# Gated linear attention and a feed-forward layer on one core: queries laid with d at partitions from the third chunk, V fetched in halves, due times of their own for chunks and weights

## The chip, the cores and the metric

One core of a Trainium2 chip runs the whole program. The metric is device microseconds of one launch. The kernel before took 511.89 us (median of 3 runs, 510.52 to 512.65). Five engines work side by side: TensorE (PE), VectorE (DVE), ScalarE (ACT), GpSimd (POOL) and SyncE (SP, which here only issues transfers). Each runs its own instructions in the order in which the program was written.

## The reference

```python
# q, k, v, alpha: (4 batches, 8 heads, 768 tokens, 48); w_in (384, 2048), w_out (2048, 384); float64 weights
for t in range(S):
    state = alpha[:, :, t, :, None] * state + einsum('bhd,bhe->bhde', k[:, :, t], v[:, :, t])
    y[:, :, t] = einsum('bhd,bhde->bhe', q[:, :, t], state)
x = y.transpose(0, 2, 1, 3).reshape(B * S, H * D)        # 3072 tokens x 384
h = x @ w_in
g = where(h >= 1, h, where(h <= -1, 0, (h + 1) ** 2 / 4))
out = g @ w_out
```

## The kernel before

The 3072 tokens are cut into 24 chunks of 128 (six to a batch). A chunk is prepared (`prepare`), attended (`attend`: `begin_chunk`, `scores`, `update`, `follow`, `outputs`, `end_chunk`) and then goes, three chunks at a time (a group, 384 columns), through the feed-forward layer: `hidden` makes the first product of a block f of 128 hidden units (nine matmuls, L912) and the activation, `second` the second product (nine matmuls, L983). There are 8 groups and 16 blocks. Both products are made of three float32r products (high x high, high x low, low x high), so operands are split into a high part (a cast on ACT) and a low part (a subtraction on DVE or POOL). The weights arrive as 64-bit words and are decoded by ACT (L368, L376, L421), DVE (L384, L395) and POOL or DVE (L408, L423); the set u serves blocks 2u and 2u+1. The first two groups share the weights: blocks 0 to 7 of group 0, the same of group 1, then blocks 8 to 15 of both.

Preparing chunk j: a, k and q are loaded (`load`, L470). The scan along time needs d at partitions. For j < EARLY = 7 the arrays are read with tokens at partitions (`tok_a`, `tok_k`, `tok_q`) and PE turns them into PSUM (`turned`, L485: four matmuls for each of a, k, q); from chunk 7 on they are read with d at partitions (`dim_...`) into SBUF. DVE scans a forward into Q (L546) and backward into inv (L572), multiplies inv by k (L588); the product Q times q (L598) is made by DVE where q lies in PSUM (chunks 1 to 6) and by POOL elsewhere, since POOL doesn't read PSUM. The keys are turned for the state's update: by PE (L662) before TURN = 10, by DVE and a round trip through DRAM (L617, L628, L638) from there. `scores` (L675) and `update` (L688, keys times V) are 32 and 32 small matmuls, `outputs` (L815) 32 to 48. V comes twice: `vt` with all heads (L507) for the update, and `both` (L518), which holds V of the other half of the chunk in 64 partitions and the state in the other 64, for the outputs. `both` has two buffers, and POOL clears it at the start (L266). `place` copies the state into `both` (ACT L707 or POOL L710). From MERGE = 6 the update and scores of chunk j and the outputs of chunk j-1 are one burst on PE.

The order on each engine is written by a planner (`Plan`): every step has an engine, an estimated duration, and a key (due time, in units of one block of a group); at each point the step that can start first goes, and of those the one with the lowest key. Some steps name a second engine (`other`). Where the planner sees PE idle for over 0.45 it puts matmuls on zeros (L1054).

Of the kernel before, what the change touches and what calls it, by code (L numbers as in the profile page):

```python
# [8 lines left out]
F32 = mybir.dt.float32  # L9
# [20 lines left out]
TURN = 10  # L30
PLACING = 4.0
MORE = 2
WARM = 15
LAG = 3.0
FETCH = 12.0
LOAD = 4.0
DECODE = 3.0
PREPARE = 2.5
MARGIN = 9.0
MARGIN0 = 9.0  # L40
MARGIN1 = 5.0
FETCH0 = 18.0
DECODE0 = 10.0
AHEAD = 15.0
FIRST = 5
ROOM = 2
LATER = 8.0
MERGE = 6
WARMTH = 165.0
HALVES = 5  # L50
QHELP = 1
HELP = 4
# [3 lines left out]
ALONE = 2  # L56

# [177 lines left out]
def gated_attention_ffn(ctx: ExitStack, tc: tile.TileContext, q, k, v, alpha, laid, out):  # L235
# [29 lines left out]
    both = const.tile([P, 2, 2, 2, G, 64], F32, name="both")  # L265
# [47 lines left out]
    with ExitStack() as main:  # L313
# [121 lines left out]
        def weights(u):  # L435
# [4 lines left out]
            fetch = key - (FETCH if u else FETCH0)  # L440
            ready = key - (DECODE if u else DECODE0)
# [13 lines left out]
            decode(u, "o", to, wo[u], ready + LAG)  # L455
# [4 lines left out]

        raws = {}

        def load(x, j, key):

            raw = raws[x, j] = buf("stage", "raw", [P, G * CH], 8)
            plan.op(
                "SP",
                Plan.ISSUE,
                key,
                lambda: nc.sync.dma_start(out=raw(), in_=laid[("tok_" if j < EARLY else "dim_") + x][j]),  # L470
                [],
                [raw],
                moved=P * G * CH * 4,
            )

        def turned(x, j, key, to=()):

            raw = raws[x, j]
            if j < EARLY:
# [17 lines left out]
        def prepare(j, key):  # L497

            early = j < EARLY
            for x in "akq":  # L500
                load(x, j, key - LOAD)
            vt = V[j] = buf("vp", "vt", [P, H, D], 2)
# [4 lines left out]
                lambda: nc.sync.dma_start(out=vt().rearrange("p h d -> p (h d)"), in_=laid["v"][j]),  # L507
                [],
                [vt],
                moved=P * DM * 4,  # L510
            )
            for r in range(2):
# [49 lines left out]
            vec(  # L562
                0.13,
                lambda: nc.vector.tensor_copy(out=inv()[:, G - 1, CH - 1 : CH], in_=bwd[:, G - 1, CH - 1 : CH]),  # L564
                ["bwd"],
                [inv],
                False,
            )
# [22 lines left out]
                j >= EARLY,  # L591
# [91 lines left out]
        def update(j):  # L683
            for g in range(G):
                for u in range(1 + ((j + 1) % PER != 0)):
                    for r in range(2):
# [4 lines left out]
                            rhs=V[j]()[halves[u], 2 * g + r],  # L691
# [4 lines left out]
        def place(i, u, key, zero=False):  # L696

            for r in range(2):
                to = both[low[r], i, r, u, :, 0:D]
                if zero:  # L700
                    plan.op("POOL", 0.15, key, lambda to=to: nc.gpsimd.memset(to, 0.0), [], [("s", i, u, r)])
                    continue
                plan.op(
                    "ACT",
                    0.36,
                    key,
                    lambda r=r, to=to: nc.scalar.copy(out=to, in_=state[low[r]]),  # L707
                    ["state"],
                    [("s", i, u, r)],
                    other=("POOL", 0.38, lambda r=r, to=to: nc.gpsimd.tensor_copy(out=to, in_=state[low[r]]), True),  # L710
                )
# [8 lines left out]
        def follow(j, key):  # L720
# [3 lines left out]
            i = j % 2  # L724
# [81 lines left out]
        def outputs(j, ps):  # L806
            n, i = group_of[j], j % 2
# [16 lines left out]
        def used(j):  # L824
            i = j % 2
# [43 lines left out]
        def attend(j, key):  # L869
# [5 lines left out]
            if j > MERGE:  # L875
                ps = ps_a(j)

                def burst(ps=ps):
# [5 lines left out]
                    "PE", 2.2, key, burst, [Q, K, ks, vt, *used(j - 1)], [*meets[j], others[j], ps], mode="quad", ends="col"  # L884
                )
                end_chunk(j - 1, ps, key)
            else:
                o = plan.op("PE", 0.55, key, lambda: scores(j), [Q, K], [*meets[j], others[j]], mode="quad")
                plan.op("PE", 0.55, key + 0.02, lambda: update(j), [ks, vt], meets[j], mode="quad", beside=True, after=[o])
# [5 lines left out]
            if (j + 1) % PER:  # L895
                place((j + 1) % 2, 0, key + 0.2)
# [164 lines left out]
        for j in range(NCH):  # L1061
# [3 lines left out]
            prepare(j, due - PREPARE - PLACING * (j >= TURN))  # L1065
# [159 lines left out]
def lay(q, k, v, alpha, w_in, w_out):  # L1225
# [57 lines left out]
```

## Time and profile before

| | |
|---|---|
| median of 3 runs | 511.89 us |
| profiled execution | 511.24 us, its span 509.5 us |
| PE busy | 494.9 us (97%) |
| DVE, ACT, POOL busy | 308.7, 312.8, 214.2 us |
| chain that ended last | PE 86%, DVE 10%, ACT 1%, issue 1% |
| granted TensorE clock | 0.998 over the span |

The shares are means over very different stretches. PE is fed by itself over most of the span; in the first 80 us DVE is at 0.9 or more of nearly every slice, and the transfers too.

### The profile page before, as it was taken

What the parts mean: (1) busy time and instruction counts of PE and PEld (TensorE: products, weight loads), DVE (VectorE), ACT (ScalarE), POOL (GpSimd) and SP (SyncE); (2) the same over time, 40 slices, a digit from 0 to 9 for tenths busy, and PEclk for the clock granted to TensorE, in tenths of its full rate; (3) what the DMA queues carried; (4) which work ended last, traced back from release to release, by engine and by line L of the source; (5) the groups of instructions that cost most, each with busy time, mean ns of one, the idle gap of its engine ahead of it and who ended that gap; (6) DMA issues with size and microseconds to landing.
All of it is one profiled execution on the core that took longest, in us unless ns stands there. A gap on an engine that the chain in (4) does not pass through costs nothing.

```text
span 509.5 us, 12191 instructions
## 1 busy us (share of the span) xinstructions
PE 494.9 (97%) x4839; PEld 477.8 (94%) x4839; DVE 308.7 (61%) x599; ACT 312.8 (61%) x611; POOL 214.2 (42%) x250
## 2 busy tenths in 40 slices
PE   8898989999999999999999999999999999999995
PEld 6787879999999999999999999999999999999994
DVE  6989998898996737457457457457457413121112
ACT  3898797786655545656555655556555655555551
POOL 3664633432255345444445434445345332333330
PEclk9999999999999999999999999999999999999999
DMA  8997957021355744344234433343213301010001
GB/s 250 376 360 234 371 166 269 9 73 53 106 170 118 218 104 120 80 116 158 58 101 129 122 105 119 77 111 122 59 37 66 110 2 21 4 48 1 0 2 51
DMA packets 59486, 59.80 MB, mean 117 GB/s; under 512 B 33600, under 2 KB 43296, under 8 KB 59424
## 3 DMA queue, kind: packets, MB, share of 16 engines
q1 hardware_dynamic: 59424, 58.97, 39.1%
q8 instruction: 40, 0.66, 0.5%
q14 instruction: 22, 0.18, 0.1%
HBM read 47.32 MB, written 9.57 MB: 112 GB/s over the span
## 4 chain that ended last, share of the span: by engine, by line
PE 86%; DVE 10%; ACT 1%; issue 1%; DVEq 0%
PE ps L983 38%; PE ps L912 38%; PE ps L815 4%; PE ps L688 2%; PE ps L675 2%; DVE inv L572 2%; DVE Q L546 2%; DVE wt L423 1%; DVE Q L761 1%; PE ps L662 1%; DVE w L395 1%; DVE inv L588 1%; PE ps L1054 1%; DVE ps L955 1%; DVE gh L962 0%
## 5 line engine op out<-in xcount | busy, mean ns | idle before, releaser
L912 PE MATMUL ps<-ring,wt 128*128 128x384 f32 (+1 forms) x1170 | 224.5, 336 | 1.1 <-DVE gh L962 1.1
L983 PE MATMUL ps<-wt,gh 128*128 128x384 f32 x1152 | 224.3, 339 | 0.0
L912 PEld LDWEIGHTS ps<-ring,wt 128*128 128x128 f32 x1170 | 204.8, 188 | 1.5 <-DVE gh L962 1.2
L983 PEld LDWEIGHTS ps<-wt,gh 128*128 128x128 f32 x1152 | 201.1, 188 | 1.4 <-POOL gh L962 0.2
L962 POOL TENSOR_TENSOR gh<-gf,gh 128x384 fp32r<-128x384 f32 x101 | 109.3, 1082 | 169.6 <-ACT gh L961 169.6
L955 DVE SCALAR_TENSOR_TENSOR gf<-gf,ps 128x384 f32<-128x384 f32 x102 | 56.2, 551 | 153.1 <-ACT gf L941 150.2
L941 ACT ACTIVATE gf<-ps,half_b 128x384 f32<-128x384 f32 (+1 forms) x130 | 75.0, 577 | 89.9 <-PE ps L912 88.6
L961 ACT CAST gh<-gf 128x384 fp32r<-128x384 f32 x102 | 52.3, 513 | 66.5 <-DVE gf L955 66.5
L941 ACT ACTIVATE gf<-gf 128x384 f32<-128x384 f32 (+1 forms) x130 | 67.7, 520 | 3.9
L408 POOL TENSOR_TENSOR w<-w,wt 128x384 int32<-128x384 int32 (+1 forms) x26 | 32.0, 1246 | 41.1 <-DVE w L395 12.9
L792 POOL TENSOR_TENSOR state<-state,last 128x192 f32<-128x192 f32 x20 | 18.6, 930 | 33.8 <-DVE state L717 33.6
L761 DVE TENSOR_TENSOR Q<-ps,mask 64x256 f32<-64x256 f32 x48 | 20.3, 423 | 14.2 <-ACT other L725 13.2
L815 PE MATMUL ps<-Q,both 128*64 128x64 f32 x372 | 26.8, 225 | 0.8 <-DVE inv L572 0.8
L815 PE MATMUL ps<-other,both 128*64 128x64 f32 x372 | 26.8, 225 | 0.0
L815 PEld LDWEIGHTS ps<-Q,both 128*64 128x64 f32 x372 | 23.5, 138 | 3.3 <-DVE inv L572 1.0
L598 POOL TENSOR_TENSOR Q<-Q,raw 128x512 f32<-128x512 f32 x18 | 23.3, 1294 | 5.0 <-DVE inv L564 2.4
L707 ACT COPY both<-state 48x192 f32<-48x192 f32 x62 | 21.6, 349 | 3.1 <-DVE state L715 0.8
L815 PEld LDWEIGHTS ps<-other,both 128*64 128x64 f32 x372 | 23.5, 138 | 0.0
L572 DVE TENSOR_TENSOR_SCAN inv<-raw,bwd 128x511 f32<-128x511 f32 x17 | 23.0, 1355 | 0.0
L546 DVE TENSOR_TENSOR_SCAN Q<-raw,fwd 128x512 f32<-128x512 f32 x17 | 20.8, 1224 | 0.2
L962 DVE TENSOR_TENSOR gh<-ps,gh 128x384 fp32r<-128x384 f32 (+1 forms) x28 | 14.6, 524 | 6.7 <-ACT gh L961 6.7
L688 PEld LDWEIGHTS ps<-vt,ks 64*64 64x64 f32 x704 | 13.3, 134 | 5.1 <-issue 4.6
(79 smaller groups left out, 447.8 us busy)
## 6 DMA issues: line engine op xcount, KB each, us to landing
both<-in_laid_v_both SPq DMA_DIRECT2D x48, 128.0 KB, 3.0
wt<-in_laid_w_in SPq DMA_DIRECT2D x8, 768.0 KB, 7.4
wt<-in_laid_w_out SPq DMA_DIRECT2D x8, 768.0 KB, 7.5
vt<-in_laid_v SPq DMA_DIRECT2D x24, 192.0 KB, 2.8
out<-ot SPq DMA_DIRECT2D x24, 192.0 KB, 2.6
raw<-in_laid_dim_a SPq DMA_DIRECT2D x17, 256.0 KB, 2.7
raw<-in_laid_dim_k SPq DMA_DIRECT2D x17, 256.0 KB, 2.7
raw<-in_laid_dim_q SPq DMA_DIRECT2D x17, 256.0 KB, 2.6
```

The lines of the kernel that those rows point to most:

```text
L408: add = lambda e, c=c: e.tensor_tensor(out=bits()[:, c], in0=bits()[:, c], in1=word(I32, 0)[:, c], op=ALU.add)
L546: lambda: nc.vector.tensor_tensor_scan(flat(Q()), aT(), flat(fwd), 0.0, ALU.mult, ALU.max),
L572: lambda: nc.vector.tensor_tensor_scan(flat(inv())[:, 0:n][:, ::-1], aT()[:, 1 : n + 1][:, ::-1], flat(bwd)[:, 0:n][:, ::-1], bwd[:, G - 1 ...
L688: nc.tensor.matmul(out=up(j, u)[64 * r : 64 * r + 64, g], lhsT=turnt[j]()[halves[u], g, 64 * r : 64 * r + 64], rhs=V[j]()[halves[u], 2 * g ...
L761: lambda r=r, u=u, to=to: nc.vector.tensor_tensor(out=to()[halves[1 - r], :, halves[u]], in0=ss(j, r)[halves[u]], in1=mask[halves[u], None ...
L815: nc.tensor.matmul(out=ps()[halves[r], to, halves[u]], lhsT=lhsT[:, r, u], rhs=x()[:, g, halves[u]], start=m + u == 0, stop=True, skip_gro ...
L912: nc.tensor.matmul(out=h(), lhsT=win(f, w)[:, kt], rhs=ring[:, at, kt, a, :], start=(m == 0), stop=(m == 3 * KT - 1),)
L941: lambda: nc.scalar.activation(out=gf(), in_=in_(), func=func, scale=scale, bias=bias),
L955: lambda: nc.vector.scalar_tensor_tensor(out=x(), in0=gf(), scalar=1.0, in1=h(), op0=ALU.min, op1=ALU.max),
L961: plan.op("ACT", 0.08 + (0.45 if x is h else 0.41) * w, key + 0.4, lambda: nc.scalar.copy(out=gh()[:, 0], in_=x()), [x], [gh])
L962: sub = lambda e: e.tensor_tensor(out=gh()[:, 1], in0=x(), in1=gh()[:, 0].bitcast(F32), op=ALU.subtract)
L983: nc.tensor.matmul(out=o_ps[seg][t](), lhsT=gh()[:, a, (t - c0) * CH : (t - c0 + 1) * CH], rhs=wout(f, w), start=(f == f0 and i == 0), sto ...
```

## The change

The loads of q switch to d at partitions from chunk 2 on (EARLYQ = 2) instead of chunk 7; a and k stay as they were (EARLYK = EARLY = 7). So the four PE transposes of q fall away for chunks 2 to 6, and Q times q of these chunks goes from DVE to POOL. The token rows that are still loaded hold 464 numbers instead of 512 (neighbouring heads overlap). `vt` holds, for each half of the tokens, only the heads that `both` doesn't hold there (96 KB instead of 192 KB), and the update reads the other half of V from `both`, which therefore gets three buffers (NB) and a longer clearing. TURN falls from 10 to 9, MERGE and HELP rise by one (HELP: chunks whose second mask is made by ACT and POOL), weight decoding on POOL is no longer split in halves (HALVES = 0). The remaining numbers move keys: SHIFT and PREP for single chunks, WFETCH, WREADY and WOUT for single weight sets. In the diff, L numbers of the changed kernel are 10 to 13 higher than those above.

```diff
+EARLYK = 7
+NB = 3
+EARLYQ = 2
-TURN = 10
-PLACING = 4.0
+TURN = 9
+PLACING = 3.0
...
-LATER = 8.0
-MERGE = 6
+LATER = 4.0
+MERGE = 7
 WARMTH = 165.0
-HALVES = 5
+HALVES = 0
 QHELP = 1
-HELP = 4
+HELP = 5
...
+SHIFT = {0: -3.0, 1: -0.5, 6: -1.0, 7: -1.5, 8: 4.5, 9: 1.0, 10: 5.5, 11: 1.5}
+WREADY = {0: -4.5, 1: 0.5, 2: -0.5, 3: -1.0, 4: 0.5, 5: -0.5, 6: -1.5}
...
-    both = const.tile([P, 2, 2, 2, G, 64], F32, name="both")
+    both = const.tile([P, NB, 2, 2, G, 64], F32, name="both")
...
+        WIDE = (G - 1) * (64 + D) + P
+        TOK = {"a": EARLY, "k": EARLYK, "q": EARLYQ}
...
-                lambda: nc.sync.dma_start(out=raw(), in_=laid[("tok_" if j < EARLY else "dim_") + x][j]),
+                lambda: nc.sync.dma_start(
+                    out=raw()[:, 0:WIDE] if j < TOK[x] else raw(), in_=laid[("tok_" if j < TOK[x] else "dim_") + x][j]
+                ),
...
-            if j < EARLY:
+            if j < TOK[x]:
...
-                            in_=raw()[:, g * P : (g + 1) * P],
+                            in_=raw()[:, g * (64 + D) : g * (64 + D) + P],
...
-            vt = V[j] = buf("vp", "vt", [P, H, D], 2)
+            vt = V[j] = buf("vp", "vt", [P, G, D], 2)
...
-            in_ps = QHELP <= j < EARLY
+            in_ps = QHELP <= j < EARLYQ
             ways = [("DVE", 0.66, lambda: mul(nc.vector), not in_ps), ("POOL", 1.3, lambda: mul(nc.gpsimd), True)]
-            (e, us, emit, port), other = ways if QHELP <= j < EARLY else reversed(ways)
+            (e, us, emit, port), other = ways if QHELP <= j < EARLYQ else reversed(ways)
...
-                            rhs=V[j]()[halves[u], 2 * g + r],
+                            rhs=V[j]()[halves[u], g] if r == u else both[halves[u], j % NB, r, u, g, 0:D],
...
-            prepare(j, due - PREPARE - PLACING * (j >= TURN))
+            due += SHIFT.get(j, 0.0)
+            prepare(j, due - PREPARE - PLACING * (j >= TURN) - PREP.get(j, 0.0))
```

On DVE, this is chunk 3 in preparation in the kernel before, from its first gate (fwd) to the products by k (inv) and q (Q), and what follows (w is a weight set being decoded, ring the split outputs of a chunk):

```order
L536 TENSOR_SCALAR fwd<-ps 128x4
L543 MEMSET ps 128x4
L546 SCALAR_TENSOR_TENSOR Q<-ps,fwd 128x512
L717 TENSOR_TENSOR state<-state,ps 128x192
L550 RECIPROCAL bwd<-Q 128x4
L564 COPY inv<-bwd 128x1
L572 SCALAR_TENSOR_TENSOR inv<-ps,bwd 128x511
L584 RECIPROCAL meet<-inv 128x4
L588 TENSOR_TENSOR inv<-inv,ps 128x512
L598 TENSOR_TENSOR Q<-Q,ps 128x512
L844 TENSOR_TENSOR ring<-ps,ring 128x3x128
L395 SCALAR_TENSOR_TENSOR w<-wt,w 128x768
```

And the same chunk on DVE in the changed kernel (L561 and L585 are the scans, L601 the product by k):

```order
L551 TENSOR_SCALAR fwd<-ps 128x4
L558 MEMSET ps 128x4
L561 SCALAR_TENSOR_TENSOR Q<-ps,fwd 128x512
L727 TENSOR_TENSOR state<-state,ps 128x192
L394 TENSOR_SCALAR w<-w 128x768
L565 RECIPROCAL bwd<-Q 128x4
L577 COPY inv<-bwd 128x1
L585 SCALAR_TENSOR_TENSOR inv<-ps,bwd 128x511
L854 TENSOR_TENSOR ring<-ps,ring 128x3x128
L597 RECIPROCAL meet<-inv 128x4
L405 SCALAR_TENSOR_TENSOR w<-wt,w 128x768
L394 TENSOR_SCALAR w<-w 128x768
```

The product by q is gone from DVE, the product by k follows only behind this piece, and the first weight set is decoded here; in the kernel before its first step stood 21 rows ahead of the piece.

On POOL the products by q of chunks 4 and 5 now stand among the decoding of the first two weight sets, each behind a low part or an addition of full width (768 columns). Before, POOL had only `last` of these chunks there, and the first sets went in halves of 384 columns.

On ACT, this follows the ninth high part of a block (L961) in the kernel before, up to the tenth:

```order
L961 CAST gh<-ps 128x384
L421 CAST wt<-w 128x768
L941 ACTIVATE gf<-ps,half_b 128x384
L941 ACTIVATE gf<-gf 128x384
L368 ACTIVATE w<-wt 128x768
L542 COPY meet<-fwd 128x4
L368 ACTIVATE w<-wt 128x768
L376 ACTIVATE wt<-wt 128x768
L961 CAST gh<-ps 128x384
```

And in the changed kernel, from the ninth to behind the eleventh (L971 is the cast; L378, L386 and L431 decode):

```order
L971 CAST gh<-ps 128x384
L431 CAST wt<-w 128x768
L951 ACTIVATE gf<-ps,half_b 128x384
L951 ACTIVATE gf<-gf 128x384
L386 ACTIVATE wt<-wt 128x768
L971 CAST gh<-ps 128x384
L951 ACTIVATE gf<-ps,half_b 128x384
L951 ACTIVATE gf<-gf 128x384
L378 ACTIVATE w<-wt 128x768
L971 CAST gh<-ps 128x384
L386 ACTIVATE wt<-wt 128x768
```

Of the sixteen L376 steps 14 stand before the ninth cast and 2 between it and the eighteenth in the kernel before; 9 and 7 in the changed one. Of the L421 steps it is 7 and 4 before, 6 and 5 now.

## Rows read from the trace of the kernel before

**Rows 1.** Stretches: length, busy us of PE, PEld, DVE, ACT, POOL; clock, DMA share, GB/s
```profile
5.00:73.00 68.00, 60.63 (x955) 52.80 (x953) 62.92 (x133) 55.74 (x109) 35.02 (x51) 1.00 0.90 299
73.00:100.00 27.00, 26.93 (x183) 26.60 (x184) 23.29 (x48) 21.35 (x41) 9.72 (x14) 1.00 0.51 171
...
130.00:504.00 374.00, 373.43 (x3432) 366.14 (x3430) 194.88 (x375) 211.00 (x418) 156.07 (x169) 1.00 0.31 83
```
**Rows 2.** Chain of waits, 0 to 84 us: start, us, what
```profile
52.20 1.15 PE ps L815 x32
...
69.14 0.66 PE ps L662 x4
...
72.54 0.48 DVE gh L962
...
73.06 1.85 PE ps L912 x9
74.92 0.61 PE ps L688 x32
```
**Rows 3.** Groups of DVE, 10 to 80 us: count, busy, mean ns
```profile
L598 DVE TENSOR_TENSOR Q<-Q,ps 128x512 f32<-128x512 f32 x6 | 4.1, 680 | 0.0
```
**Rows 4.** Timeline of DVE, 30 to 82 us: start, us
```profile
32.55 0.68 DVE L598 TENSOR_TENSOR Q<-Q,ps 128x512 f32<-128x512 f32 x1
33.15 0.55 DVE L844 TENSOR_TENSOR ring<-ps,ring 128x384 fp32r<-128x384 f32 x1
...
49.45 0.86 DVE L761 TENSOR_TENSOR other<-ps,mask 64x256 f32<-64x256 f32 x2
```
**Rows 5.** Timeline of PE, 97 to 105 us
```profile
99.14 0.60 PE L662 MATMUL ps<-ident,inv 128*128 128x128 f32 x4
99.50 1.81 PE L983 MATMUL ps<-wt,gh 128*128 128x384 f32 x9
...
102.82 0.68 PE L688 MATMUL ps<-vt,ks 64*64 64x48 f32 x32
...
104.99 0.44 PE L983 MATMUL ps<-wt,gh 128*128 128x384 f32 x1
```
**Rows 6.** Timeline of ACT, 10 to 75 us
```profile
44.57 0.83 ACT L421 CAST wt<-w 128x768 fp32r<-128x768 f32 x1
...
59.33 1.74 ACT L376 ACTIVATE wt<-wt 128x768 int32<-128x768 uint32 x2
```
**Rows 7.** Groups of POOL over the span
```profile
L598 POOL TENSOR_TENSOR Q<-Q,raw 128x512 f32<-128x512 f32 x18 | 23.3, 1294 | 5.0 <-DVE inv L564 2.4 <-PE ps L675 1.9 <-ACT raw L596 0.5
...
L408 POOL TENSOR_TENSOR w<-w,wt 128x768 int32<-128x768 int32 x6 | 11.5, 1909 | 20.1 <-ACT ks L665 8.6 <-ACT gf L941 7.6 <-DVE w L395 4.0
```
**Rows 8.** The line L588: duration ns min/median/max
```profile
L588 DVE TENSOR_TENSOR inv<-inv,raw x17: 691/1112/1683, 85.0 to 391.5; 128x512 f32<-128x512 f32 x17
L588 DVE TENSOR_TENSOR inv<-inv,ps x7: 686/689/689, 8.8 to 68.4; 128x512 f32<-128x512 f32 x7
```
**Rows 9.** Timeline of POOL, 0 to 90 us
```profile
1.02 1.80 POOL L266 MEMSET both<- 128x2048 f32 x1
2.86 0.29 POOL masks.py:199 TENSOR_SCALAR_AFFINE_SELECT ident<-ident 128x128 f32<-128x128 f32 x1
```
**Rows 10.** Timeline of SP, 0 to 6 us (issues)
```profile
2.85 1.21 SPq L518 DMA_DIRECT2D both<-in_laid_v_both  x2
4.11 0.59 SPq L470 DMA_DIRECT2D raw<-in_laid_tok_a  x1
```
**Rows 11.** Timeline of PE, 0 to 12 us
```profile
1.06 3.38 PE L1054 MATMUL ps<-zeros 128*128 128x256 bf16 x15 [1.06 <-DVE zeros L249]
4.24 2.67 PE L485 MATMUL ps<-ident,raw 128*128 128x128 f32 x12
...
8.81 1.28 PE L485 MATMUL ps<-ident,raw 128*128 128x128 f32 x8 [0.37 <-DMA raw<-in_laid_tok_a]
```

More of the change, by code (lines that the diff above doesn't have):

```diff
@@ L506, in prepare @@
                 key - LOAD + 1,
[L507 removed]
+                lambda: nc.sync.dma_start(out=vt().rearrange("p g d -> p (g d)"), in_=laid["v"][j]),
                 [],
                 [vt],
[L510 removed]
+                moved=P * DM * 2,
             )
@@ L518, in prepare @@
                     lambda r=r, rows=rows: nc.sync.dma_start(
-                        out=both[rows, j % 2, r].rearrange("p u g e -> p (u g e)"), in_=laid["v_both"][j, rows]
+                        out=both[rows, j % NB, r].rearrange("p u g e -> p (u g e)"), in_=laid["v_both"][j, rows]
                     ),
                     [],
-                    [("v", j % 2, u) for u in range(2)],
+                    [("v", j % NB, u) for u in range(2)],
                     moved=P * DM * 4 * 2 // 3,
@@ L561, in prepare @@
             )
[L562 to L568, printed above, removed]
+            last_col = lambda e: e.tensor_copy(out=inv()[:, G - 1, CH - 1 : CH], in_=bwd[:, G - 1, CH - 1 : CH])
+            if TAIL and early:
+                plan.op("POOL", 0.22, key, lambda: last_col(nc.gpsimd), ["bwd"], [inv], port=True)
+            else:
+                vec(0.13, lambda: last_col(nc.vector), ["bwd"], [inv], False)
             n = G * CH - 1
@@ L702, in place @@
                     continue
[L703 to L711, printed above, removed]
+                ways = [
+                    ("ACT", 0.36, lambda r=r, to=to: nc.scalar.copy(out=to, in_=state[low[r]]), False),
+                    ("POOL", 0.38, lambda r=r, to=to: nc.gpsimd.tensor_copy(out=to, in_=state[low[r]]), True),
+                ]
+                (e, us, emit, port), other = reversed(ways) if key < PLACE else ways
+                plan.op(e, us, key, emit, ["state"], [("s", i, u, r)], port=port, other=None if key < PLACE else other)
         def grow(j, u, key):
@@ L883, in attend @@
                 plan.op(
-                    "PE", 2.2, key, burst, [Q, K, ks, vt, *used(j - 1)], [*meets[j], others[j], ps], mode="quad", ends="col"
+                    "PE", 2.2, key, burst, [Q, K, ks, vt, ("v", j % NB, 0), ("v", j % NB, 1), *used(j - 1)], [*meets[j], others[j], ps], mode="quad", ends="col"
                 )
@@ L895, in attend @@
             if (j + 1) % PER:
-                place((j + 1) % 2, 0, key + 0.2)
+                place((j + 1) % NB, 0, key + 0.2)
         def hidden(n, f, key, c0=0, c1=GROUP):
@@ L1237, in lay @@
         x = x.reshape(B, H, S // CH, CH, D)[..., e]
-        laid["tok_" + name] = x.transpose(0, 2, 3, 1, 4).reshape(NCH, CH, H * 64)
+        t = x.transpose(0, 2, 3, 1, 4).reshape(NCH, CH, G, 2 * 64)
+        laid["tok_" + name] = np.concatenate([t[:, :, :-1, : 64 + D].reshape(NCH, CH, -1), t[:, :, -1]], axis=2)
         x = x.reshape(B, G, 2, S // CH, CH, 64)
         laid["dim_" + name] = x.transpose(0, 3, 2, 5, 1, 4).reshape(NCH, P, G * CH)
-    x = v.reshape(B, H, S // CH, CH, D)
-    laid["v"] = x.transpose(0, 2, 3, 1, 4).reshape(NCH, CH, DM)
+    x = v.reshape(B, G, 2, S // CH, 2, HC, D)
+    x = np.stack([x[:, :, u, :, u] for u in range(2)], axis=3)
+    laid["v"] = x.transpose(0, 2, 3, 4, 1, 5).reshape(NCH, CH, G * D)
     x = v.reshape(B, G, 2, S // CH, 2, HC, D)[:, :, ::-1].transpose(0, 3, 2, 5, 4, 1, 6).reshape(NCH, P, 2, G, D)
```

41 lines of the change are left out of this document (23 added, 18 removed).

## The prediction, blind

> **What bounds the kernel now.** I read the slices first, then the busy time by stretches, then the chain of waits, then the timelines where the chain leaves PE. The reader is to see two regimes. From about 73 us on PE is busy for 26.93 of 27.0 us and then for 373.43 of 374.0 [rows 1]: no wait is left there, and only PE's own work or a new wait can change the time. Before, from 5 to 73 us, PE is busy for 60.63 of 68 us, part of it on zeros, while DVE is busy for 62.92 [rows 1]. That is 93%, and the chain shows that it is DVE that PE waits for: the eighth block's first product stands at 73.06 because its PSUM bank is freed by the low part that DVE makes at 72.54 (L962), and the keys at 69.14 wait for DVE's product by k in the same way [rows 2]. The first product at 73.06 is the last one with a wait ahead of it in the chain; call it the gate. What moves the gate moves the end, unless the dense stretch behind it loses it again. ACT has 55.74 us of the 68 and POOL 35.02: POOL has room, ACT a little. The clock is 1.00 in all three stretches [rows 1], the upper of TensorE's two levels, so no gain or loss is looked for there.
>
> **Part by part.** All sums are made against the profiled execution, 511.24 us, which is 0.65 below the median of 511.89 and within the runs shown.
>
> *Products by q.* Six of them stand on DVE before [rows 3], one in the changed order (chunk 1). One runs 680 ns, but the next DVE instruction starts 0.60 us behind it (32.55 to 33.15 [rows 4]); so 5 x 0.60 = 3.0 us leave DVE ahead of the gate. *Second masks* of chunk 4 (HELP): two instructions of 0.43 [rows 4], 0.87 us. Counted through the order, these seven are what DVE has less up to the tenth block's low part for good; one scan and one subtraction of a weight set are only put off behind it, and I count no gain for them. DVE is busy 93% of the time, so nearly all of the 3.9 us should reach the gate: **-3.9 us**. From both sides: 0 if other waits take the place, and up to -9.0 if the 5.1 us in which DVE stands idle (68 less 62.92) went too.
>
> *PE's transposes of q.* Twenty matmuls fewer, all ahead of the gate, where PE waits for DVE or runs on zeros. DVE's relief already holds the gain, so they count nothing more.
>
> *PE behind the gate.* In the changed order the update of chunk 6 stands ahead of the gate; in the old one it comes right behind it (0.61 us at 74.92 [rows 2]). The outputs of chunk 6 come out of the burst with chunk 7: before, the burst of update, scores and outputs takes 2.17 us (102.82 to 104.99 [rows 5]); now the outputs alone take 1.15 (52.20 [rows 2]) and update and scores the other 1.02. So that part stays at 2.17, and the 0.61 us go. The keys of chunk 9 leave PE (TURN): 0.36 us (99.14 to 99.50 [rows 5]). Together **-1.0 us**, since PE has no idle time there.
>
> *What comes in for the keys of chunk 9* is one more DVE transpose and five more transfers, where DVE has 179 us of room (374 less 194.88 [rows 1]). Fourteen chunks take this way already without a wait on PE in that stretch. I cost it at nothing; if its keys came late, the burst and all behind it would wait, one landing at most, about 2 us.
>
> *ACT behind the gate.* This is where I see a price. Five L376 steps and one L421 move from ahead of the ninth cast to between the ninth and the eighteenth, that is into the stretch 73 to 100 us; by 0.87 and 0.83 [rows 6] they are 5.2 us, less two small steps that leave, some 4.6. ACT has 27 - 21.35 = 5.65 us idle there [rows 1], in pieces, so the work fits with 1 us to spare, if every piece can be used. Bounds: nothing, or the whole 4.6. I take **+1.2**, nearer to nothing, because four buffers of gf and gh let ACT lag behind PE by more than one block. DVE gets only the put-off scan and subtraction, about 2 us, and has 3.7 idle there: nothing.
>
> *POOL.* It gains five products of 1.29 us [rows 7], 6.5 us, of 33 idle (68 less 35.02 [rows 1]). Full-width decoding takes 1.91 us in one piece [rows 7] instead of two halves of about half that. Nothing, while the products come before their scores; the rival below prices the other case.
>
> *The start.* POOL's clearing of `both` takes 1.80 us [rows 9] and becomes half as long again, 2.70. The unit matrix for the first transposes would then be ready at about 4.05 instead of 3.15 [rows 9]; PE's run on zeros ends at 1.06 + 3.38 = 4.44 [rows 11], which hides it with 0.4 to spare. SP's fifth transfer waits for the clearing (2.85 [rows 10]) and everything behind it on that queue is issued 0.9 later, chunk 1's gates first (4.11 [rows 10]); PE waits for them at 8.81 already, for 0.37 [rows 11]. Against that, the transfers up to and with it are 1280 KB instead of 1472 (four token arrays of 232 KB, once 256; `vt` 96, once 192; `both` 256), which at the 299 GB/s of the first 68 us [rows 1] is 0.6 earlier. I cost the rest at nothing, with 0 to +0.9 as bounds.
>
> *Shorter token rows, half of vt, update reading `both`.* The chain of waits names no transfer up to 84 us, so less to move gives nothing by itself; the update now also waits for the `both` of its chunk, loaded beside `vt`. Nothing, up to +0.9 with the start.
>
> *Due times* only reorder; their effect is in the counts above.
>
> Sum: -3.9 - 1.0 + 1.2 = -3.7, so 511.24 - 3.7 = **507.5 us**, 0.9% below the median shown.
>
> One rule of the Trainium skill speaks against the move to POOL. The line L588 runs in 686 to 689 ns while k lies in PSUM, and in 691 to 1683 ns with both inputs in SBUF [rows 8]: something holds it up by as much as 0.99 us, and only in the second case. The Trainium skill (SBUF — State Buffer, section "Who interferes with whom") says that a DVE instruction with two SBUF inputs and a GpSimd instruction that reads SBUF exclude each other, the later one waiting for the whole of the other; rows 8 agree. What that would do here is the third rival.
>
> **The rivals.**
> 1. *The relief is larger* (0.13): part of DVE's 5.1 us of idle goes too, since chunks 2 to 6 come earlier and their waits overlap, and ACT finds room. Say 2.5 us of it, without the 1.2: 511.24 - 3.9 - 1.0 - 2.5 = 503.8. For it: twenty transposes less on PE between DVE's steps. Against: DVE's idle time lies in many short pieces.
> 2. *ACT takes the bound behind the gate* (0.19): the 4.6 us find no room, since ACT's idle pieces wait for PE and DVE themselves: 511.24 - 4.9 + 4.6 = 510.9, no change. For it: 21.35 of 27 us busy; against: the buffers.
> 3. *POOL's products hold up DVE* (0.05): each of the five stands against a DVE step with two SBUF inputs (the decoding) for 0.99 us [rows 8]: 507.5 + 5.0 = 512.5, no change. Against: most DVE steps of that stretch read PSUM.
> 4. *Slower: POOL's queue gates the scores* (0.08). For chunks 3 to 6 the product by q stands behind a full-width addition, which waits for DVE's decoding. If the scores of each wait for one such addition and the product itself, 1.91 + 1.29 = 3.2 us for each of four chunks, with the masks, the state and the outputs behind them, that is 12.8, and with a third of it hidden by DVE's other work 8.5: 507.5 + 8.5 = 516.0. It decides for slower from 7.0 us on (514.45 less 507.5). For it: the order on POOL. Against: 33 us of idle time there, and a product of chunk 4 that needs to be ready only at its scores, some fillers later in PE's order.
>
> **How the numbers follow.** The forecast's family has 0.55, of which I put 0.08 at or above 509.33. 0.5% (2.56 us) is about what a measurement of this kernel can tell from no change: faster is below 509.33, slower above 514.45. Faster: 0.47 + 0.13 = 0.60; same: 0.08 + 0.19 + 0.05 = 0.32; slower 0.08. The range goes from rival 1 to a little above rival 2: 503.8 to 512. Above it stand rival 4 and most of rival 3, below it little: 1 to 2 in 10.
>
> **What would show it.** Right: PE dense from about 69 us instead of 73; DVE's products by q one instead of six in front of it, and DVE still at 0.9 or more there; the scores of chunks 2 to 6 not waiting for POOL. ACT wrong or right: its idle time in the 27 us behind the gate is about 1 us, and PE shows waits for ACT (gf or gh) there if rival 2 holds. Rival 3: decoding steps on DVE that become longer than before beside POOL's products. Rival 4: scores released by POOL's product, PE idle ahead of them. The start is wrong if chunk 1's first transposes come later than 9.2. The forecast as a whole is wrong if PE becomes dense no earlier than 73 us, or if new waits appear behind 130 us.

## The result and the profile after

The changed kernel took 506.32 us in the median of 4 runs (505.61 to 507.91), the kernel before 512.22 us (4 runs): ratio 0.9894, 95% interval 0.9867 to 0.9921. Timed a second time it came to 506.59 us, ratio 0.9895 (0.9872 to 0.9919). So the gain is about 5.4 us. The profiled execution took 505.61 us, with a span of 503.9 us where the one before had 509.5.

These are the stretches of the changed kernel, with the columns of [rows 1]. The first goes to 69 us, since the gate lies earlier now.

```profile
5.00:69.00 64.00, 58.99 (x975) 52.87 (x974) 59.42 (x129) 51.40 (x106) 41.08 (x49) 1.00 0.93 303
...
73.00:100.00 27.00, 27.00 (x215) 26.66 (x214) 23.98 (x43) 25.59 (x46) 9.94 (x8) 1.00 0.46 137
100.00:130.00 30.00, 30.00 (x174) 30.00 (x173) 26.34 (x44) 22.59 (x43) 12.40 (x8) 1.00 0.16 49
130.00:499.00 369.00, 367.12 (x3395) 359.42 (x3393) 191.92 (x366) 202.85 (x397) 155.91 (x177) 1.00 0.31 82
```

PE is full from 73 to 130 us. DVE is as crowded ahead of the gate as it was (59.42 of 64 us, 93%). ACT has 25.59 of the 27 us behind it, as forecast, and PE still waits for nothing there. Behind 130 us PE has 1.88 us less than the 369, but 1.15 of that lies behind its last product, since the span ends earlier; what is new is one wait of 0.73 us, shown below. (The 0.57 of [rows 1] too lie at the end of the span.)

The chain of waits of the same profile (start, us, what) no longer runs through DVE alone:

```profile
1.08 2.60 POOL both L276
...
4.33 0.58 SPq L533
...
6.06 4.33 DMA raw<-in_laid_tok_q
...
10.93 6.70 DMA wt<-in_laid_w_in
...
45.24 0.84 ACT wt L431
...
60.69 0.70 DVE ring L854
...
61.44 3.39 PE ps L922 x18
64.83 0.23 PE ps L1064 x2
65.06 3.19 PE ps L993 x18
68.26 1.58 PE ps L922 x9
```

The last wait ends at 61.44. The product that stood at 73.06 [rows 2] is now the one at 68.26, so the gate is 4.80 us earlier; in the second profile of the same kernel it is at 68.71. The head of the chain is now POOL's clearing of `both`, SP's queue behind it and the landing of the first weights; then ACT and DVE take turns.

At the start, the timeline of PE shows that chunk 1's first transposes come at 8.38 instead of 8.81 [rows 11], and that they wait longer:

```profile
4.23 2.21 PE L500 MATMUL ps<-ident,raw 128*128 128x128 f32 x12
...
8.38 1.26 PE L500 MATMUL ps<-ident,raw 128*128 128x128 f32 x8 [1.07 <-DMA raw<-in_laid_tok_a]
```

The new wait behind 130 us is one. PE's timeline:

```profile
159.50 0.69 PE L922 MATMUL ps<-ring,wt 128*128 128x384 f32 x3
160.92 6.03 PE L922 MATMUL ps<-ring,wt 128*128 128x384 f32 x33 [0.73 <-DMA ring<-ring]
```

and SP's issues ahead of it:

```profile
153.75 2.53 SPq L870 DMA_DIRECT2D ring<-ring  x3
156.33 1.54 SPq L1023 DMA_DIRECT2D ot<-sums  x3
157.91 1.88 SPq L870 DMA_DIRECT2D ring<-ring  x3
```

Six transfers move rows of the ring (L870), three loads of earlier sums (L1023) stand in their midst, and PE waits for the last of the six.

### The profile page after: what moved, and what is told of

Its sections match the earlier page's. It is cut to its first block, busy times and chain, and to the rows that moved or that the text cites. A ratio compares the mean times of both kernels' runs of the same rounds, so it can differ in the third digit from the quotient of the medians.

```text
span 503.9 us, 12162 instructions
## 1 busy us (share of the span) xinstructions
PE 491.0 (97%) x4817; PEld 475.7 (94%) x4817; DVE 306.3 (61%) x588; ACT 307.4 (61%) x598; POOL 225.8 (45%) x255
## 4 chain that ended last, share of the span: by engine, by line
PE 87%; DVE 4%; DMA 3%; ACT 3%; SPq 1%; issue 1%; POOL 1%; DVEq 0%; POOLq 0%
PE ps L922 39%; PE ps L993 39%; PE ps L825 4%; PE ps L701 2%; PE ps L688 2%; DMA wt<-in_laid_w_in 1%; DMA raw<-in_laid_tok_q 1%; DMA ring<-ring 1%; POOL both L276 1%; DVE Q L771 0%; DVE w L405 0%; DVE inv L585 0%; DVE w L394 0%; ACT ring L849 0%; SPq L870 0%
## 5 line engine op out<-in xcount | busy, mean ns | idle before, releaser
L971 ACT CAST gh<-gf 128x384 fp32r<-128x384 f32 x102 | 52.3, 512 | 62.9 <-DVE gf L965 62.8
L418 POOL TENSOR_TENSOR w<-w,wt 128x768 int32<-128x768 int32 x16 | 31.3, 1956 | 34.1 <-ACT gf L951 8.0
L611 POOL TENSOR_TENSOR Q<-Q,raw 128x512 f32<-128x512 f32 x23 | 30.0, 1306 | 6.2 <-DVE bwd L565 3.8
L585 DVE TENSOR_TENSOR_SCAN inv<-raw,bwd 128x511 f32<-128x511 f32 x17 | 23.6, 1387 | 0.0
L561 DVE TENSOR_TENSOR_SCAN Q<-raw,fwd 128x512 f32<-128x512 f32 x17 | 20.7, 1220 | 0.2
L717 ACT COPY both<-state 48x192 f32<-48x192 f32 x49 | 17.1, 350 | 1.6 <-DVE state L725 0.5
L854 DVE TENSOR_TENSOR ring<-ps,ring 128x512 fp32r<-128x512 f32 (+1 forms) x24 | 16.1, 672 | 3.0 <-ACT ring L849 2.3
```

The costliest lines, as they stand in the source:

```text
L418: add = lambda e, c=c: e.tensor_tensor(out=bits()[:, c], in0=bits()[:, c], in1=word(I32, 0)[:, c], op=ALU.add)
L561: lambda: nc.vector.tensor_tensor_scan(flat(Q()), aT(), flat(fwd), 0.0, ALU.mult, ALU.max),
L585: lambda: nc.vector.tensor_tensor_scan(flat(inv())[:, 0:n][:, ::-1], aT()[:, 1 : n + 1][:, ::-1], flat(bwd)[:, 0:n][:, ::-1], bwd[:, G - 1 ...
L611: mul = lambda e: e.tensor_tensor(out=flat(Q()), in0=flat(Q()), in1=qT(), op=ALU.mult)
L971: plan.op("ACT", 0.08 + (0.45 if x is h else 0.41) * w, key + 0.4, lambda: nc.scalar.copy(out=gh()[:, 0], in_=x()), [x], [gh])
```

## The experiments

| kernel | median us (runs) | ratio to before, 95% interval | gate us |
|---|---|---|---|
| before | 511.4 to 512.2 | 1 | 73.06 |
| after | 506.32 (4) | 0.9894 (0.9867 to 0.9921) | 68.26 |
| after_again | 506.59 (6) | 0.9895 (0.9872 to 0.9919) | 68.71 |
| e1_q_on_dve | 507.35 (6) | 0.9903 (0.9879 to 0.9927) | 71.17 |
| e8_q_on_dve_twice | 511.72 (12) | 1.0001 (0.9990 to 1.0012) | 74.26 |
| e6_dve_less | 506.01 (5) | 0.9902 (0.9886 to 0.9918) | 68.80 |
| b1_q_out | 511.65 (12) | 0.9993 (0.9976 to 1.0010) | 74.05 |
| b2_q_and_turns_out | 512.04 (12) | 1.0006 (0.9985 to 1.0027) | 74.2 |
| e2_q_by_pe | 514.39 (12) | 1.0041 (1.0019 to 1.0063) | 75.4 |
| e3_old_due | 511.00 (12) | 0.9980 (0.9963 to 0.9998) | 75.3 |
| e5_no_own | 509.29 (11) | 0.9956 (0.9942 to 0.9969) | 69.85 |
| e7_act_more | 506.84 (6) | 0.9917 (0.9899 to 0.9936) | 69.6 |
| e4_clear_late | 505.44 (6) | 0.9869 (0.9840 to 0.9897) | 67.73 |
| best | 504.62 (5) | 0.9862 (0.9840 to 0.9883) | 67.72 |

The gate is the start of the same product in each profile, by the chain of waits (with one decimal where the chain doesn't stop at it, from the records of PE); one profile stands behind each, so differences of half a microsecond there mean nothing. The kernel before was timed beside the others on three occasions, with medians of 512.21, 511.4 and 511.62 us; ratios are the ones to compare.

### How much of it is DVE's relief

**e1_q_on_dve** gives the products by q back to DVE, in the changed order.

```diff
-            plan.op(e, us, key + 0.3, emit, [Q, qt, last], [Q], port=port, other=None if in_ps else other)
+            o = plan.op(e, us, key + 0.3, emit, [Q, qt, last], [Q], port=port, other=None if in_ps else other)
+            if 2 <= j < 7:
+                o.instead = lambda: mul(nc.vector)
...
-                o.emit()
+                getattr(o, "instead", o.emit)()
```

> The changed kernel in its own order; only the products by q of chunks 2 to 6 go back to DVE, at the place in the order where POOL made them. They then read two inputs in SBUF, so one takes 0.69 us or more. Theory (what DVE is spared before the gate is the gain): five products of 0.60 to 1.0 us come back onto DVE ahead of the gate, +3 to +5 us: 509.3 to 511.3 us, the gate at 71 to 73 us instead of 68.3. Rival (the new order and due times are the gain, DVE has room): at most +1 us, 506.3 to 507.3, the gate within 1 us of 68.3.

Measured: 507.35 us, ratio 0.9903 beside 0.9894 and 0.9895, so 0.4 to 1.0 us slower by ratios and medians; the intervals overlap. Its one profile has the gate at 71.17 and took 508.26 us, above its median. By its time it lies between the two expectations, nearer to the rival: most of the gain stays without POOL's help. The gate, in the one profile, lies in the range of the theory, 2.5 to 2.9 us later than in the changed kernel.

**e8_q_on_dve_twice** has each of these products twice on DVE.

```diff
+                o.instead = lambda: (mul(nc.vector), mul(nc.vector))
```

> The changed kernel in its own order; the products by q of chunks 2 to 6 are made by DVE instead of POOL, and each is done twice (so the output differs): ten instructions of 0.6 to 0.7 us more on DVE ahead of the gate than in the changed kernel, five more than where they were done once (507.35 us). Theory (what DVE does ahead of the gate comes out one for one): 3.0 to 3.5 us above the single ones, 510.3 to 511. Rival (DVE has slack there, since the single ones cost 1.0 instead of 3.0): at most 1.2 us above, 507.4 to 508.6.

Measured: ratio 1.0001, 0.0098 or 5.0 us above the single ones and 5.4 above the changed kernel. The whole gain is gone; ten instructions of 0.69 us on DVE cost 5.4. The largest of PE's waits from 20 to 75 us (line, what it waited for: us, times, longest) is for DVE's product by k:

```profile
PE ps L677 <- DVE inv L601: 3.2, 2, 1.8
```

So DVE's load matters here: the first 3 us cost 1 at most, the next 3 more than they last.

**e6_dve_less** goes the other way.

```diff
-                plan.op(
+                o = plan.op(
                     "DVE",
                     0.52,
...
+                if u < 3:
+                    o.instead = lambda: None
```

> The changed kernel in its own order; the six shifts (line L394) of the first three weight sets are left out, so the weights decoded from them are not the reference's. DVE is spared 6 x 0.50 = 3.0 us ahead of the gate, as much as the change itself took from it with the products by q. Theory (DVE still holds the gate): 2 to 3 us faster, 503.3 to 504.3 us, the gate at 65.3 to 66.3 instead of 68.3. Rival (after the change transfers, ACT and PE's own order hold it as much): at most 1 us faster, 505.3 to 506.5.

Measured: ratio 0.9902, gate 68.80: nothing gained. Its chain of waits shows what stands there instead:

```profile
39.94 7.75 DMA wt<-in_laid_w_in
...
47.71 6.44 DMA raw<-in_laid_dim_k
```

From 40 to 54 us it is transfers: a weight set and then a k. In the first profile of the changed kernel the chain runs through DVE and ACT there, in the second (after_again, below) through the same two transfers. One thing clouds the gate of this run: its granted clock is 0.52 from 11 to 14 us and 0.92 in the 3 us behind, which is at most 3 x 0.48 + 3 x 0.08 = 1.7 us of PE's work. The times don't hang on that: the run with the highest granted clock (0.999) is the longest of the five, 507.37 us.

**b1_q_out** tests the prediction's first step where it was made: in the kernel before, with its order.

```diff
+            if 2 <= j < 7:
+                o.instead = lambda: None
```

> The kernel before in its own order, without the five products by q of chunks 2 to 6 on DVE (so the scores of these chunks lack q). Nothing else differs. Theory of the prediction (DVE's relief reaches the gate one for one): 3.0 us faster than the kernel before, ratio 0.993 to 0.995. Rival (something else, such as transfers or PE's own order with its zeros, stands close behind DVE): at most 1.2 us faster, ratio 0.998 to 1.000.

Measured: 0.9993 (0.9976 to 1.0010). The rival holds. DVE's timeline in this kernel says how:

```profile
26.05 1.18 DVE L384 TENSOR_SCALAR w<-w 128x768 int32<-128x768 int32 x1 [0.34 <-ACT w L368]
...
35.96 0.49 DVE L964 TENSOR_TENSOR gh<-ps,gh 128x128 fp32r<-128x128 f32 x2 [1.34 <-ACT gh L963]
...
47.34 1.22 DVE L546 TENSOR_TENSOR_SCAN Q<-ps,fwd 128x512 f32<-128x512 f32 x1
...
58.72 0.35 DVE L719 TENSOR_TENSOR state<-state,ps 128x192 f32<-128x192 f32 x1 [2.38 <-PE ps L690]
```

and the same steps in the kernel before:

```profile
26.41 0.55 DVE L384 TENSOR_SCALAR w<-w 128x768 int32<-128x768 int32 x1
...
35.91 0.49 DVE L962 TENSOR_TENSOR gh<-ps,gh 128x128 fp32r<-128x128 f32 x2 [0.94 <-ACT gh L961]
...
47.33 1.22 DVE L546 TENSOR_TENSOR_SCAN Q<-ps,fwd 128x512 f32<-128x512 f32 x1
...
57.14 0.35 DVE L717 TENSOR_TENSOR state<-state,ps 128x192 f32<-128x192 f32 x1 [0.26 <-PE ps L688]
```

Three products have been left out ahead of the scan (24.35, 32.55 and 44.20 us in the kernel before), 1.8 us, and the scan stands where it stood. The time goes piece by piece: at 26.05 DVE waits 0.34 us for ACT, and the step itself takes 1.18 instead of 0.55 (why, no run shows); at 35.96 it waits 1.34 us for ACT instead of 0.94. A step at 57.14 waits for PE's update (L688) already in the kernel before, so what DVE has gained by then on the fourth product goes to PE. ACT has little idle time in the stretch from 20 to 50 us (kernel before, columns of [rows 1]):

```profile
20.00:50.00 30.00, 26.49 (x457) 22.75 (x454) 27.45 (x60) 28.23 (x58) 17.69 (x25) 1.00 0.92 303
```

ACT had 28.23 of these 30 us, 94%, more than DVE; it has 28.01 here. Its share of 82% over 5 to 73 us [rows 1], from which the prediction read "a little" room, hid that. The page of the kernel before shows it too: in the first seven of its 40 slices DVE is busy for 6, 9, 8, 9, 9, 9 and 8 tenths (not 0.9 in nearly every one, as was said ahead of the prediction), ACT for 3, 8, 9, 8, 7, 9 and 7. Behind 50 us a second thing eats into this profile:

```profile
50.00:53.00 3.00, 1.41 (x30) 1.21 (x32) 2.81 (x7) 0.60 (x2) 0.34 (x1) 0.99 0.80 330
53.00:56.00 3.00, 3.00 (x25) 2.88 (x22) 3.00 (x7) 1.74 (x4) 1.29 (x4) 0.50 1.02 426
56.00:59.00 3.00, 3.00 (x59) 2.70 (x58) 0.62 (x2) 2.36 (x5) 2.01 (x2) 0.94 1.02 362
```

PE was busy for 1.41 of 3 us, and then TensorE's granted clock was 0.50, its lower level, for about 3 us: 3 x 0.50 + 3 x 0.06 = 1.7 us of PE's work at the most; PE's update, and with it the step at 58.72, is 1.58 us later than in the kernel before. Yet the kernel before has the same idle time in the same place, and its clock stayed up:

```profile
50.00:53.00 3.00, 1.43 (x30) 1.22 (x32) 2.81 (x7) 0.50 (x2) 0.34 (x1) 1.00 1.01 414
53.00:56.00 3.00, 3.00 (x36) 2.68 (x34) 3.00 (x7) 2.55 (x5) 1.29 (x4) 1.00 0.95 353
```

So this loss belongs to the execution and not only to the edit. It does not hide the 3.0 us: of the runs with a granted clock of 0.997 or more over the span, the three of this kernel took 510.25 to 510.50 us, the ten of the kernel before that were timed beside it 510.38 to 511.84, in the median 511.2. That is a gain of about 0.9 us, from few runs, and still in the rival's range.

**b2_q_and_turns_out** leaves out the twenty transposes too.

```diff
+                if x == "q" and 2 <= j < 7:
+                    flips[j].instead = view
```

> As the one before, and without PE's twenty transposes of q for chunks 2 to 6 as well: 20 x 0.109 = 2.2 us less on PE ahead of the gate. Theory of the prediction (PE waits for DVE there, so its own work counts nothing): as without the products alone, within 0.5 us. Rival (PE's own work ahead of the gate counts): up to 2.2 us faster than without the products alone.

Measured: 1.0006 (0.9985 to 1.0027), no better than without the products alone. The prediction's "they count nothing more" holds in the old order. Both savings together, 3.0 us of DVE and 2.2 of PE, give nothing that can be told from zero there. (Its profile has the same fall of the clock, 0.50 from 53 to 56 us; its two runs at 0.997 or more took 509.61 and 510.14.)

### What the order is worth

**e3_old_due** has the new structure and the old numbers.

```diff
-TURN = 9
+TURN = 10
...
-MERGE = 7
+MERGE = 6
-HALVES = 0
+HALVES = 5
-HELP = 5
+HELP = 4
...
-SHIFT = {0: -3.0, 1: -0.5, 6: -1.0, 7: -1.5, 8: 4.5, 9: 1.0, 10: 5.5, 11: 1.5}
+SHIFT = {}
```

> The structure of the changed kernel (q with d at partitions from chunk 2, V in halves, shorter rows, three buffers of both) with all numbers of the planner as before (TURN 10, MERGE 6, HELP 4, HALVES 5, the old margins, no times for single chunks or weights). Theory (relief of DVE is what counts): the five products are off DVE, the two second masks are not, so about 3.0 of the gain of 5.6 us stay: 508 to 509.5 us. Rival (the due times are the gain): 511 to 513, no better than the kernel before. A third way: the old numbers fit the new structure badly, and it is slower than before: above 513.

Measured: 0.9980 (0.9963 to 0.9998), 1.0 us faster than before. In microseconds that is the lower edge of the rival's range, though just told apart from no gain: 4.4 of the 5.4 us hang on the numbers. In its order PE has 125 runs on zeros instead of 103 before and 105 after; the weight loads of zeros for them:

```profile
L1064 PEld LDWEIGHTS <-zeros x125: 95/98/151, 1.1 to 79.9; 128*128 128x128 bf16 x125
```

That is 22 runs on zeros more than before, where twenty transposes have gone.

**e5_no_own** keeps the general numbers (TURN, MERGE, HELP, HALVES and margins such as AHEAD, which goes from 15 to 23) and empties the five tables.

```diff
-SHIFT = {0: -3.0, 1: -0.5, 6: -1.0, 7: -1.5, 8: 4.5, 9: 1.0, 10: 5.5, 11: 1.5}
+SHIFT = {}
...
-WREADY = {0: -4.5, 1: 0.5, 2: -0.5, 3: -1.0, 4: 0.5, 5: -0.5, 6: -1.5}
+WREADY = {}
```

> The changed kernel with all its general numbers, but without the times of single chunks and weight sets (SHIFT, PREP, WFETCH, WREADY and WOUT empty); the order is made anew. Theory of the prediction (due times only reorder and count nothing): no worse than 1 us above the changed kernel, 506 to 507.5 us. Rival (since all numbers as before gave 511.0, the gain hangs on the numbers, and on those of single chunks and sets above all): 509 to 511.

Measured: 0.9956 (0.9942 to 0.9969), the rival. The times of single chunks and sets are worth 0.0061 or 3.1 us. Its gate is at 69.85, 1.6 behind that of the changed kernel; the rest is lost behind it, part of it in a wait that neither the kernel before nor the changed one has there (PE's waits, 90 to 499 us):

```profile
PE ps L701 <- DMA ks<-blocks: 1.2, 2, 0.9
```

**e2_q_by_pe** keeps all new numbers and undoes the layout of q.

```diff
-EARLYQ = 2
+EARLYQ = 7
```

> The changed kernel with EARLYQ = 7: chunks 2 to 6 load token rows of q, PE transposes them (20 matmuls more), DVE makes the product by q from PSUM, and the order is made anew with the changed numbers; halved V, shorter rows, three buffers of both and all due times stay. Theory (relief of DVE): five products of 0.60 us come back, +3.0 to +3.9 us and up to 2 more for PE's transposes and their PSUM banks: 509.3 to 512. Rival (due times, halved V and shorter rows are the gain): 506 to 508.

Measured: 1.0041 (1.0019 to 1.0063), 2.1 us slower than before and 7.5 slower than the changed kernel: more than either theory gave. The windows show a good part of it:

```profile
38.00:41.00 3.00, 0.03 (x2) 0.00 (x0) 2.83 (x7) 2.71 (x5) 2.49 (x3) 0.88 1.06 332
41.00:44.00 3.00, 2.72 (x68) 2.39 (x68) 2.89 (x6) 2.87 (x6) 1.35 (x4) 0.50 1.02 405
44.00:47.00 3.00, 3.00 (x47) 2.32 (x44) 2.52 (x7) 1.43 (x4) 2.70 (x3) 0.50 0.48 141
...
68.00:71.00 3.00, 3.00 (x11) 3.00 (x11) 2.71 (x3) 2.02 (x3) 2.11 (x2) 0.50 0.53 106
...
171.00:174.00 3.00, 3.00 (x12) 3.00 (x12) 0.93 (x3) 1.10 (x2) 0.00 (x0) 0.60 0.79 237
```

PE stands still there, waiting 3.3 us for DVE's product by k; then the granted clock is 0.50 for 6 us, and again for 3 at 68 us, behind a wait of 2.6 us for DVE's product by q: 9 x 0.50 = 4.5 us of PE's work at the most. A third fall, behind a wait of 2.2 us for the ring, is at 0.83 from 168 and 0.60 from 171 us, 1.7 us more at the most. Nothing fills the first wait, and this order has fewer runs on zeros:

```profile
L1064 PEld LDWEIGHTS <-zeros x76: 96/98/152, 1.1 to 44.8; 128*128 128x128 bf16 x76
```

The clock was low in all twelve runs, 0.984 to 0.992 in the mean over the span, where the kernel before had 0.989 to 0.999 beside them. The means are 0.989 and 0.9955, so the clock costs at most 0.0068 x 512 = 3.5 us, an estimate. The loss of 2.1 us may thus be the clock's altogether; that the gain is missing is not. So the new numbers without the new layout of q are no gain.

### ACT, the start and the new wait

**e7_act_more** loads ACT behind the gate.

```diff
+TWICE = 9, 13
...
                 o.emit()
+                if getattr(o, "scaled", False):
+                    scaled += 1
+                    if TWICE[0] <= scaled <= TWICE[1]:
+                        o.emit()
```

> The changed kernel in its own order; five of ACT's scalings of weights (line L378), those between 73 and 100 us, are done twice: 5 x 0.83 = 4.2 us more for ACT where it has 1.4 us idle. Theory of rival 2 and of the term of 1.2 us (what finds no idle time there comes out as PE's waits): 2.7 to 4.2 us slower, 509.0 to 510.5. Other theory (the activations' buffers and the weights' lead carry ACT's lag, and so the term was nothing): at most 0.5 us, 506.3 to 506.8.

Measured: 506.84 us, 0.9917 (0.9899 to 0.9936): 1.1 us by the ratios, 0.3 to 0.5 by the medians, far from 2.7. The gate of its profile, 69.6, stands ahead of the first doubled step (75.14), so that it is later is not the edit's doing. Its windows:

```profile
73.00:100.00 27.00, 27.00 (x214) 26.66 (x214) 22.61 (x38) 26.60 (x46) 10.12 (x8) 1.00 0.49 153
100.00:130.00 30.00, 29.78 (x170) 29.46 (x170) 25.44 (x46) 25.54 (x50) 13.06 (x8) 1.00 0.16 49
```

ACT goes to 26.60 of 27 us and carries the rest over: 25.54 in the next 30 us instead of 22.59, 1.01 + 2.95 = 4.0 of the 4.2 us added. (The fifth doubled step came at 103.06.) PE is full to 100 us and idle for 0.22 behind. The term of 1.2 us was nothing. Much more would not have fitted: in this profile the chain that ended last runs through ACT up to 100.44 us.

**e4_clear_late** clears one buffer of `both` at once, two later.

```diff
-    nc.gpsimd.memset(both, 0.0)
+    nc.gpsimd.memset(both[:, 0:1], 0.0)
...
+    nc.gpsimd.memset(both[:, 1:NB], 0.0)
```

> The changed kernel in its own order; only the first of the three buffers of both is cleared ahead of the unit matrix and the mask, the other two behind them. SP's fifth transfer and all behind it are then issued about 1.7 us earlier. Theory of the prediction (the start costs nothing): 506.3 us within 0.5. Rival (the longer clearing heads the chain that ends last, through SP's queue and the first weights): 0.9 to 1.7 us faster, 504.6 to 505.4, and the gate as much earlier than 68.3.

Measured: 505.44 us, 0.9869 beside 0.9895: some 1.0 us faster, gate 67.73. The intervals overlap, but the same edit in the last kernel below gives the same gate. SP's fifth transfer goes at 2.68 instead of 3.70, 1.0 us earlier and not 1.7:

```profile
2.68 1.22 SPq L534 DMA_DIRECT2D both<-in_laid_v_both  x2
```

The edit takes 1.7 us off the clearing ahead of it, while the change had added 0.8 (2.60 against 1.80 [rows 9]); and it brings the fifth transfer forward by 1.02 us, where the change had put it back by 0.85 (3.70 against 2.85 [rows 10]). So between half and four fifths of that gain, 0.5 to 0.8 us, is what the change had lost at the start, an estimate by proportion.

**after_again** is the changed kernel once more, beside the later kernels.

> The changed kernel as it is, so that it is timed on the same chip as the others of this call: 506.3 us, ratio 0.989 to the kernel before, within 0.003. The gate in a second profile: at 68.3 within 1 us if the profile shown is typical; up to 2 us later if it was a lucky one (its time was the lowest of four).

Measured: 506.59 us, 0.9895, gate 68.71. Its chain of waits from 39 to 54 us:

```profile
38.60 8.54 DMA wt<-in_laid_w_in
47.15 6.84 DMA raw<-in_laid_dim_k
```

Those are transfers, where the first profile's chain goes through ACT and DVE: two executions of one program, and a different one of the close bounds came last.

**best** adds to the late clearing that SP issues the sums behind the ring.

```diff
+            for i in reversed(range(len(ops))):
+                if getattr(ops[i], "row", "") == "sums":
+                    rest = [k for k in range(i + 1, min(i + 40, len(ops))) if ops[k].engine == "SP"][:6]
+                    rings = [k for k in rest if getattr(ops[k], "row", "") == "ring"]
+                    if rings:
+                        ops.insert(rings[-1], ops.pop(i))
```

> The changed kernel in its own order with two edits: the second and third buffer of both are cleared behind the unit matrix (alone 0.9869 of the kernel before), and on SP's queue the loads of the sums (L1023) that stood among the six transfers of the ring at 156 us go behind them. The ring's last transfer is then issued 1.6 us earlier, and the wait of 1.0 us at 159.5 goes: 0.9 us less than with the late clearing alone, 504.0 to 504.8 us, ratio 0.985. If the transfers of that queue only change places and another becomes late: no gain, ratio 0.987.

Measured: 504.62 us, 0.9862 (0.9840 to 0.9883), the fastest of all and clearly ahead of the kernel before, but not told apart from the late clearing alone (0.9869). PE's timeline:

```profile
158.97 6.42 PE L924 MATMUL ps<-ring,wt 128*128 128x384 f32 x36
165.62 0.62 PE L995 MATMUL ps<-wt,gh 128*128 128x384 f32 x2 [0.24 <-ACT gh L973]
166.76 1.49 PE L995 MATMUL ps<-wt,gh 128*128 128x384 f32 x7 [0.51 <-POOL gh L974]
```

The wait for the ring is gone (33 products had been cut off from 3), and 7 us later PE waits 0.24 for ACT and 0.51 for POOL. So a later step takes the place of part of it, and the two profiles' spans (502.2 and 502.6 us) show no gain.

## Why the prediction came out, and where its reasons failed

The time was 507.5 predicted and 506.32 measured, the gain 3.7 us against 5.6 us in the profiles. The direction and the stretch that moved were right. That the number came out is in part luck: the largest term was put down to DVE alone, which by itself gives next to nothing, and the price of 1.2 us was none. The terms, one by one:

- **DVE's relief, -3.9.** The gate did move, by 4.80 and 4.35 us in two profiles. But the sentence "DVE is busy 93% of the time, so nearly all of the 3.9 us should reach the gate" failed: three quarters of that relief, put into the kernel before by itself, gave 0.9993 (b1). ACT stood beside DVE, busy for 28.23 of 30 us from 20 to 50 us, and PE's update behind that; DVE came to wait for them instead, and the chain of waits shows only the one that came last. What holds is narrower: DVE's load is one condition, since 6.9 us put back take the whole gain (e8), but neither the first 3 us back (e1) nor 3 us less (e6) moved the time by more than about 1 us.
- **Due times, nothing by themselves.** Wrong. With the old numbers 1.0 us of the gain is left (e3), without the times of single chunks and sets 2.3 (e5). The prediction had read their effect from the order, but booked it under DVE; the counts came out near the truth, the cause did not.
- **ACT behind the gate, +1.2.** The row came out as foreseen (1.41 us idle of 27), the price did not: PE waited for nothing there, and 4.2 us more on top cost PE 0.22 us to 130 us (e7). Lag on ACT went into the weights' lead and was worked off later. The other side of the move was not counted at all: the same steps left the stretch ahead of the gate. Busy time from 0 to the gate shows it (columns of [rows 1]; the kernel before, b1, the changed kernel, e1, e8):

```profile
0.00:73.06 73.06, 64.57 (x972) 55.81 (x972) 64.76 (x137) 57.27 (x111) 38.02 (x62) 1.00 0.87 292
```
```profile
0.00:74.05 74.05, 65.94 (x973) 57.05 (x973) 62.81 (x131) 56.82 (x110) 38.31 (x62) 0.98 0.84 287
```
```profile
0.00:68.26 68.26, 62.19 (x987) 55.17 (x988) 60.46 (x131) 52.41 (x107) 44.13 (x60) 1.00 0.90 292
```
```profile
0.00:71.17 71.17, 63.18 (x987) 55.63 (x988) 63.41 (x136) 52.64 (x107) 37.59 (x55) 1.00 0.85 281
```
```profile
0.00:74.26 74.26, 63.90 (x987) 55.81 (x988) 66.86 (x141) 52.64 (x107) 37.66 (x55) 1.00 0.81 270
```

With less on DVE and ACT nearly as before, the gate doesn't come earlier (b1). With 4.6 us less on ACT it is at 71.17 or 74.26, as DVE has 1.35 less than before or 2.10 more (e1, e8). With 4.3 less on DVE and 4.9 less on ACT it is at 68.26. On the straight line between e1 and e8, DVE's old load would go with a gate at 72.4, an estimate: either relief alone moves the gate by little, the two together by 4.8. The ratio on the same line, 0.994, would keep 3.0 of the 5.4 us, more than that gate explains; so the share of each stays open. It is argued from these runs: none took ACT's load alone away, and the orders differ in more than these two loads.
- **PE behind the gate, -1.0.** From gate to the end of the span it is 0.80 us less in one profile and 0.25 in the other; a new wait of about 1 us for the ring at 159 us, lies in both. The prediction had named new waits behind 130 us as a sign that the forecast as a whole is wrong; this one it did not foresee, and it costs little. Without that wait, 0.73 and about 1.0 us, PE's own saving is 1.5 and 1.25, somewhat more than the 1.0 forecast.
- **PE's transposes, nothing more.** Right in the old order (b2). In e3's order there are 22 more runs on zeros.
- **The start, nothing, 0 to +0.9.** The unit matrix was hidden as forecast. But the longer clearing delays SP's queue, and it heads the chain in the changed kernel: about +0.5 to +0.8 by e4's proportions, inside the bounds. The sign named for it, transposes later than 9.2, was a bad one: they came at 8.38, earlier than before though they were issued later, and e4 has them at 7.97. That fewer bytes stood ahead of them is the likely reason; no run tests it alone.
- **POOL, nothing.** Right: no wait of PE names POOL's product. Rival 4 is out. Rival 3, which leaned on the Trainium skill (SBUF — State Buffer, section "Who interferes with whom"), is out for this order: the decoding on DVE took no longer than before (958 ns in the median in both, 1141 at the longest before).

```profile
L405 DVE SCALAR_TENSOR_TENSOR w<-wt,w x16: 931/958/983, 25.8 to 122.0; 128x768 int32<-128x768 int32 x16
```

In e3's order the same line has one of 1722 ns, at 26.41 us, while POOL is in a subtraction that reads SBUF (L433, 25.35 to 27.32); so lengthening like that of [rows 8] is there when such steps meet, and the changed order has none on this line.

- **Rivals 1 and 2.** Rival 1 (503.8, a larger relief without the 1.2) was nearer in kind than its chance of 0.13 said: without the price on ACT the forecast's own sum is 506.3. Rival 2 fell with e7.

What stays open: which of the single due times carry the 3.1 us, and how much of the gate's move is ACT's relief and how much DVE's.

## What to carry to other kernels

A chain of waits names one engine, but read each other engine's busy time over the 30 us that the chain covers, not over the whole ramp: here ACT was at 94% where the average said 82%, and 3 us taken from DVE alone gave nothing that could be told from zero. Work moved out of a crowded stretch can count twice, as relief where it leaves and as a price where it lands, and the price is only what no buffer or lead can carry. The new structure with the old numbers gave 1.0 us, the new numbers without the new layout of q gave none, and both together gave 5.4: undo each alone before saying which one did it.

## What the runs showed of the hardware

TensorE's granted clock fell to 0.50 for 3 to 6 us after stretches in which PE had stood (busy 1.41 of 3 us in b1, 0.03 of 3 us in e2), and it cost at most 1.7 us in b1 and 4.5 us in the first 75 us of e2. It did not fall each time: the kernel before has 1.43 of 3 us in the place of b1's 1.41, and its profile shows 1.00 there. The twelve runs of b1 have 0.990 to 0.999 in the mean over the span. A wait of PE in the ramp can so cost more than it lasts, and it seems to do so in some executions of a kernel and not in others. The order with fewer runs on zeros (76 instead of 105, e2) had the lower clock in all of its twelve runs; that the zeros are the cause is not shown.
